# Attention and a squared-ReLU MLP on one core: a new order for the attention stage's list of steps, with other ranks, engine letters and buffer homes

## The chip, the cores and the metric

The kernel runs on one core of a Trainium2 chip. The core has five engines that run side by side, each through its own queue in order: TensorE (PE in the profile), VectorE (DVE), ScalarE (ACT), GpSimd (POOL) and SyncE (SP), which here only issues transfers. The time is device microseconds (us) of one execution, and the figure that counts is the median of several.

## The reference

Attention with a compressive memory, for 4 batches, 8 heads, 576 positions and 64 columns a head, and behind it an MLP on the 2304 x 512 result:

```python
scores = scale * q @ k.T                      # causal, S = 576, D = 64
a      = softmax(scores)                      # over the keys
local  = a @ v
q_p    = where(q > 0, q, exp(q) - 1) + 1
mem    = (q_p @ M_prev) / (q_p @ z_prev + 1e-6)
x      = g * mem + (1 - g) * local            # g = sigmoid(beta), one per head
h      = x @ w_in                             # 2304x512 @ 512x2048
y      = (s * relu(h) ** 2 + b) @ w_out       # 2304x2048 @ 2048x512
```

## The kernel before

**Stages.** PE does three things one after the other. First comes the attention stage: 16 pairs of heads (pair g is batch g // 4, heads 2p and 2p+1), and in among them the first 41 blocks of `x @ w_in`. It ends at 282 us. Then come the other blocks of `x @ w_in`, up to about 367 us, and then the product with `w_out` (lines 800 to 904). Only the first stage is planned from a list of steps; the other two are loops written out by hand.

**A pair in the attention stage.** Three *visits* of PE (four for pair 0) make the scores (`scores`, L383) in two halves of PSUM called S buffers. DVE masks them, copies them out and takes row minima (`red`, L390). ACT takes exponentials and row sums (`ex`, L396). DVE adds the sums and inverts them (L435, L436), and DVE or POOL scales the rows (`scale`, L402). Beside this the memory term is made from the q rows (`phi`: `RELU` L319 to L323, exponential L324, DVE L325, `ZMUL` L329, DVE L331 to L335, `PUTS` L342). PE transposes both in four *banks* (`bank`, L463) into PSUM buffers called T, of which there are four, each bank taking two. ACT or DVE copies the banks out (`copy`, L472 to L479). PE makes the pair's result (`second`, L514), and ACT and DVE split it into a high and a low part `xs` (L535, L536). `x @ w_in` is done in three matmuls of such parts (`mm1`, L580 to L582), and `w_in`, which arrives as 64-bit numbers, is turned into a high and a low part in 20 *pieces* (`convert`, L558 to L573; pieces 0 to 7 are 256 columns wide, the others 512).

**What sets the order.** `Plan.add` takes a step with an engine, a cost, a rank, what it reads and writes, and PSUM buffers that it takes and gives. `Plan.deal` then plays the steps through in a model of the engines: at each turn the engine that is free first takes the step with the lowest rank among those that are ready. The resulting order is written out as it is; each engine's queue on the chip holds the instructions in that order, and on the chip each waits for what it really needs. In the model a transfer lands 1.9 us after its last byte is sent, POOL's steps and the DVE steps marked `port` never overlap, and PE changes from blocks of `x @ w_in` ("full") to attention work when a ready attention step has waited `HOLD` or the ready ones add up to `WORK`; both have an early and a late value, and `TURN` is the model's time at which the late one begins.

**Matmuls that only keep PE running.** `warm(n, ps)` (L270) issues n matmuls of a zero tile; each is two instructions in the trace, all of line 272. `WARM` of them open the kernel. `FILL` has the number that follows each of pair 0's four visits. `Plan.waits` adds more wherever the model sees PE idle for over a microsecond and a PSUM buffer free.

**The numbers of a pair.** `AT[g]` is the rank r0 from which all ranks of pair g count: loads r0 - 4 to r0 - 1, `red` r0 + 0.1 - `UR`, `ex` r0 + 0.15, `scale` r0 + `RC`, transposes r0 + `RT`, copies r0 + `RT` + 0.1 - `UC`, result r0 + `RA`, `xs` r0 + `RX` - `UX`; `RPS` and `RQS` place the two halves of the memory term. `RELU`, `ZMUL`, `PUTS`, `COPY` and `SCAL` name the engine of a step for each pair (A, D, P for ACT, DVE, POOL; in `SCAL` one letter for each of the five row tiles, in `COPY` one for each bank), `HIGH` and `LOW` that of each piece's two parts. `W0` to `WS` are the ranks of the pieces, `WL` how far ahead of its rank a piece's load stands. `JOIN[g]` says which banks of a pair are transposed as one step (a: banks 0 and 3; b: banks 1 and 2; c: both). `HOME[m]` is the kind of PSUM buffer for block m, T or S. The first `EARLY` blocks of batch 0 run their first half as soon as pairs 0 and 1 are done.

All visits also write a common key `"visit"`, so that they stand in the list in the order of the pairs, whatever their ranks. The blocks of `x @ w_in` are chained in the same way, by `"seq"`.

Of the kernel before, what the change touches and what calls it, by code (L numbers as in the profile page):

```python
# [43 lines left out]
class Plan:  # L44
# [5 lines left out]
    LAT = 0.17  # L50
    RATE = 220.0e3
    SWITCH = {"full": 0.22, "row": 0.13, "col": 0.13}
    TURN = 80
    HOLD, WORK, WAIT = (2.5, 3), (0.5, 4), (0.15, 0.05)
    FREE = {"DVE": 0.05, "POOL": 0.10}

    def __init__(self, **pools):
# [20 lines left out]
    def deal(self):  # L78
        ready = {}
        clock = {}  # L80
        wire = port = 0.0
# [11 lines left out]
        while any(ready.values()):  # L93
            best = None
            for eng, some in ready.items():
# [16 lines left out]
                if eng == "PE":  # L112
                    late = t0 >= self.TURN
                    wait = 0.15 if mode == "full" else self.WAIT[late]
# [9 lines left out]
                t, s = min(now, key=lambda x: (x[1]["rank"], x[1]["n"]))  # L124
# [3 lines left out]
            t, s = best  # L128
# [7 lines left out]
                port = max(port, s["end"] - self.FREE[s["eng"]])  # L136
            if s["bytes"]:
                wire = max(wire, t) + s["bytes"] / self.RATE
                s["end"] = wire + 1.9
            for place, pool in s["take"]:  # L140
                f = self.free[pool]
                k = min((k for k in range(len(f)) if f[k] is not None), key=lambda k: f[k])
# [29 lines left out]
def attention_moe_kernel(  # L172
# [116 lines left out]

    plan = Plan(S=2, T=4)  # L290
    plan.idle = "TS", 0.3, lambda n, pool, k: warm(n, TB[k] if pool == "T" else SB[k])
    WARM, FILL = 7, (3, 4, 2, 6)
    UR, UC, UX = 0.6, 1, 0
    RP, RC, RT, RA, RX = 0.9, 0.5, 1.4, 2.4, 2.3
    RPS = [0.6, 0.6, 0.6, 0.4, -0.5, 0.6, 0.2, 0.4, ] + [0.4] * 8
    RQS = [0.7, 0, 0.9, 0.5, 0.9, -1.5, -1, -1, ] + [0.3] * 8
    RSR, WL = 0.6, 2
    RELU = "DPAAADDAPPAAAAAA"
    ZMUL = "DDPPDDDPPPPPPPPP"
    PUTS = "PDPDPDDDPPPPPPPP"  # L300
    COPY = ["AADA", "DAAD", "AAAD", "AAAA", "AAAA", "AADA", "AAAA", "DAAD", "DAAD", "AADA", ] + ["AAAD"] * 6
    SCAL = ["DPPPP", "PPPPP", "DPPPP", "DDDDD", "DPPPP", "DDPPP", "PPPPP", "PPPDD", "PPDDD", "PPPPP", ] + ["PPPPP"] * 6
    HIGH, LOW = "APAAAAAAAPAAAAAAPPPP", "DPDDDDPDDDDDPPDDDDDP"
    PARTS = "3232333222222222"
    AT = [-0.3, 1.8, 4.4, 5.7, 9.3, 10.8, 12.9, 16.2, 20.5, 22.5, 26.4, 27.1, 39.1, 40.0, 41.8, 46.8]
    W0, W1, W2, W3, WA, WB, WC, WD, WS = 5, 6.6, 6, 6.5, 8.5, 9, 12, 0.4, 0.4

    def phi(g):
        b, p = divmod(g, NP)
# [8 lines left out]
        if RELU[g] == "A":  # L318
            add("ACT", 0.72, lambda: nc.scalar.activation(PHR, q, AF.Relu), r0 + RPS[g], [("q", u)], ["phr"])  # L319
        elif RELU[g] == "D":  # L320
            add("DVE", 0.45, lambda: nc.vector.tensor_scalar(PHR, q, 0.0, None, ALU.max), r0 + RPS[g], [("q", u)], ["phr"], port=True)
        else:
            add("POOL", 0.88, lambda: nc.gpsimd.tensor_scalar(PHR, q, 0.0, None, ALU.max), r0 + RPS[g], [("q", u)], ["phr"])  # L323
        add("ACT", 0.72, lambda: nc.scalar.activation(q, q, AF.Exp), r0 + RPS[g] + 0.01, [], [("q", u)])  # L324
        add("DVE", 0.73, lambda: nc.vector.scalar_tensor_tensor(q, q, 1.0, PHR, ALU.min, ALU.add), r0 + RPS[g] + 0.1,  # L325
            ["phr"], [("q", u)], port=True)
        side = lambda c: (("POOL", nc.gpsimd), ("DVE", nc.vector))[c == "D"]
        ez, mul = side(ZMUL[g])
        add(ez, 1.54 if ez == "POOL" else 0.83, lambda: mul.tensor_mul(  # L329
            PHR, q, z.unsqueeze(1).to_broadcast([128, 5, 2, D])), r0 + RQS[g] + 0.01, [("q", u), ("z", u)], ["phr"], port=True)  # L330
        add("DVE", 0.73, lambda: nc.vector.tensor_reduce(n, PHR, AX.X, ALU.add), r0 + RQS[g] + 0.02, ["phr"], [("n", u)])  # L331
# [290 lines left out]
            tick()  # L622

    LEFT = 7
    HOME = "TTTTTTTTTTTSTTTSTTTTTSSSTSTTTTTTTTSSSTTTT"
    JOIN = "00000000c0000aa0"
    EARLY = 2
    MM = [(b, f) for b in range(B - 1) for f in range(NF - LEFT * (b == 2))]
    WRANK = [W0, W1, W2, W3] + [WA + WD * k for k in range(4)] + [WB + WD * k for k in range(4)] + [
        WC + WS * k for k in range(8)]  # L630
# [322 lines left out]
```

## Time and profile before

| | |
|---|---|
| time, median of 3 runs (lowest to highest) | 553.13 us (551.82 to 553.98) |
| the profiled execution: its time, and its span | 551.54 us, 549.8 us |
| PE busy, share of the span | 539.8 us, 98% |
| ACT busy, share | 398.8 us, 73% |
| DVE busy, share | 392.4 us, 71% |
| POOL busy, share | 273.2 us, 50% |

The span runs from the first to the last instruction; the 1.7 us by which the time is longer lie around it. An engine is busy while one of its instructions runs; PE's busy time also holds the matmuls that only keep it running. "Idle before" is time in which an engine stood still ahead of an instruction, with the engine that released it.

### The profile page before, as it was taken

Reading aid. Unit: us, or ns where it says so; the run is one execution under the profiler, and the core shown is the slowest. Engines: PE = TensorE matmul, PEld = TensorE weight load, DVE = VectorE, ACT = ScalarE, POOL = GpSimd, SP = SyncE. Lnnn points to the kernel's source line nnn. Section 1 sums busy time; section 2 is a strip of 40 time slices with the busy share of each in tenths; the row PEclk is TensorE's granted clock in tenths of the full one; section 3 lists DMA queues with packets and bytes.
Section 4 is the critical chain, followed back from the end, with each engine's and each line's share of the span. In section 5 each row is a group of like instructions: output and inputs, shape, how many; then the busy total and the mean of one; then the engine's idle time right before and its main releaser. Section 6 shows DMA issues by size and latency. Waiting matters only on the chain.

```text
span 549.8 us, 11492 instructions
## 1 busy us (share of the span) xinstructions
PE 539.8 (98%) x4104; PEld 445.5 (81%) x4104; DVE 392.4 (71%) x971; ACT 398.8 (73%) x877; POOL 273.2 (50%) x279
## 2 busy tenths in 40 slices
PE   9899999999999999999999999999999999999997
PEld 7666677777777777777788888889999999999996
DVE  5899999999666455234009979344798898888872
ACT  5999899974788747646325668969987977887840
POOL 3773454567756653454000000327578668768760
PEclk9999999999999999999999999999999999999999
DMA  6645686645444342321148574649335344353101
GB/s 184 197 141 162 195 267 189 219 152 173 134 165 131 101 136 98 106 78 45 58 142 356 168 252 153 204 159 301 106 107 163 117 128 150 106 163 116 39 30 38
DMA packets 56665, 81.50 MB, mean 148 GB/s; under 512 B 7584, under 2 KB 39072, under 8 KB 56608
## 3 DMA queue, kind: packets, MB, share of 16 engines
q1 hardware_dynamic: 54064, 78.63, 44.2%
q10 hardware_dynamic: 2544, 2.14, 1.2%
q8 instruction: 32, 0.52, 0.4%
q14 instruction: 25, 0.20, 0.1%
HBM read 57.15 MB, written 23.59 MB: 147 GB/s over the span
## 4 chain that ended last, share of the span: by engine, by line
PE 89%; DVE 7%; POOL 1%; DMA 1%; issue 1%; ACT 0%; DVEq 0%; POOLq 0%
PE yps L808 12%; PE yps L812 11%; PE sb L514 7%; PE sb L383 7%; PE tb L580 6%; PE hps L580 5%; PE hps L581 5%; PE hps L582 5%; PE tb L463 5%; PE yps L811 5%; PE yps L810 5%; PE tb L581 5%; PE tb L582 5%; DVE P L390 2%; PE tb L514 2%; PE sb L580 2%
## 5 line engine op out<-in xcount | busy, mean ns | idle before, releaser
L402 POOL TENSOR_SCALAR P<-P,sr,omg 128x576 f32<-128x576 f32 (+4 forms) x130 | 90.7, 712 | 56.2 <-DVE sr L436 21.6
L812 PE MATMUL yps<-rb,op 128*128 128x256 f32 x360 | 101.1, 281 | 0.0
L396 ACT ACTIVATE P<-P,mn 128x64 f32<-128x64 f32 (+4 forms) x160 | 88.7, 560 | 17.0 <-DVE mn L390 16.4
L390 DVE CUSTOM_DVE_ANT_0 P<-sb,mask 128x64 f32<-128x64 f32 (+4 forms) x160 | 71.4, 483 | 21.0 <-PE sb L383 20.8
L808 PE MATMUL yps<-rb,op 128*128 128x512 f32 x216 | 76.9, 396 | 0.0
L812 PEld LDWEIGHTS yps<-rb,op 128*128 128x128 f32 x360 | 67.9, 189 | 0.0
L788 POOL TENSOR_TENSOR sum<-src 128x512 f32<-128x512 f32 x10 | 13.0, 1296 | 103.4 <-ACT src L772 88.7
L383 PE MATMUL sb<-qk 64*128 64x288 f32 (+4 forms) x384 | 57.0, 409 | 0.2 <-DMA qk<-in_qk_t_dram 0.2
L796 POOL TENSOR_TENSOR op<-src,op 128x512 fp32r<-128x512 f32 x30 | 43.5, 1470 | 16.9 <-ACT op L795 16.8
L819 DVE TENSOR_TENSOR yu<-yu,yps 128x256 f32<-128x256 f32 x90 | 36.5, 414 | 19.8 <-PE yps L812 18.8
L463 PEld LDWEIGHTS tb<-ident,P 64*128 64x128 f32 x928 | 37.2, 139 | 14.6 <-issue 4.8
L808 PEld LDWEIGHTS yps<-rb,op 128*128 128x128 f32 x216 | 40.6, 188 | 9.0
L463 PE MATMUL tb<-ident,P 64*128 64x64 f32 x928 | 43.2, 227 | 3.3 <-DVE xs L536 1.3
L383 PEld LDWEIGHTS sb<-qk 64*128 64x128 f32 x384 | 35.7, 188 | 12.8 <-issue 6.8
L810 PE MATMUL yps<-rb,op 128*128 128x256 f32 x144 | 40.5, 281 | 0.0
L811 PE MATMUL yps<-rb,op 128*128 128x256 f32 x144 | 40.5, 281 | 0.0
L795 ACT CAST op<-src 128x512 fp32r<-128x512 f32 x50 | 30.3, 615 | 11.5 <-PE yps L812 9.8
L796 DVE TENSOR_TENSOR op<-sum,op 128x512 fp32r<-128x512 f32 x36 | 37.1, 1032 | 0.8 <-ACT op L795 0.7
L472 ACT COPY pt<-tb 128x512 f32<-128x512 f32 x58 | 31.2, 588 | 7.7 <-PE tb L463 7.5
L796 POOL TENSOR_TENSOR op<-w1H,op 128x512 fp32r<-128x512 f32 x24 | 34.9, 1484 | 0.0
L587 ACT ACTIVATE r<-hps 128x256 f32<-128x256 f32 x62 | 21.5, 388 | 16.4 <-DMA r_d<-r 13.3
L396 ACT ACTIVATION_READ_ACCUMULATOR P<-P,mn 128x1 f32 x160 | 31.2, 195 | 0.0
(172 smaller groups left out, 1550.0 us busy)
## 6 DMA issues: line engine op xcount, KB each, us to landing
r_d<-r SPq DMA_DIRECT2D x41, 256.0 KB, 2.3
src<-r_d SPq DMA_DIRECT2D x20, 512.0 KB, 4.6
qk<-in_qk_t_dram SPq DMA_DIRECT2D x15, 576.0 KB, 4.1
raw<-in_moe_w_out_dram SPq DMA_DIRECT2D x16, 512.0 KB, 6.8
w1H<-r_d SPq DMA_DIRECT2D x16, 512.0 KB, 4.5
xa<-in_moe_w_in_dram SPq DMA_DIRECT2D x12, 512.0 KB, 5.1
r_d<-r SPq DMA_DIRECT2D x48, 128.0 KB, 2.3
qs<-in_q_rows_dram SPq DMA_DIRECT2D x16, 320.0 KB, 3.7
```

The source lines that it names most:

```text
L383: nc.tensor.matmul(at(ps, j, o, n), lhsT=qk[rs, 128 * i:128 * i + 128], rhs=qk[rs, S + 64 + c0:S + 64 + c0 + n], start=True, stop=True, ti ...
L390: nc.vector.tensor_tensor_reduce(P[:, j, PB[i] + 64:PB[i] + 64 + n], at(ps, j, o, n), m, -SCALE, 3.0e38, ALU.add, ALU.min, mn[:, j, i:i + 1])
L396: nc.scalar.activation(pt, pt, AF.Exp, scale=-1.0, bias=mn[:, j, i:i + 1], accum_out=sm[:, j, i, 0:1])
L402: e.tensor_scalar(pt, pt, sr[:, j, i:i + 1], omg[:, h:h + 1], ALU.mult, ALU.mult)
L463: nc.tensor.transpose(TB[ps[h]][:, o[h]:o[h] + 64], P[rs, j, c:c + 128], ident[rs, rs], tile_position=(64 * h, 0))
L580: nc.tensor.matmul(ps, lhsT=wH[:, p, fs], rhs=xs[:, 0], start=p == 0, stop=False)
L581: nc.tensor.matmul(ps, lhsT=wH[:, p, fs], rhs=xs[:, 1], start=False, stop=False)
L796: (nc.gpsimd if m in ONPOOL else nc.vector).tensor_sub(L, x, H.bitcast(F32))
L808: nc.tensor.matmul(tile, lhsT=H, rhs=B, start=f == 0, stop=False)
L810: nc.tensor.matmul(ps, lhsT=H, rhs=B[:, 0], start=f == 0, stop=False)
L811: nc.tensor.matmul(ps, lhsT=H, rhs=B[:, 1], start=False, stop=False)
L812: nc.tensor.matmul(ps, lhsT=L, rhs=B[:, 0], start=False, stop=f == KF - 1)
```

## The change

The model of transfers lands them half a microsecond later (2.4 in place of 1.9 us behind the last byte), two rules for PE's change between kinds of work are loosened, pair 0's `FILL` matmuls are taken out, and nearly all ranks, engine letters and homes are replaced. With them `Plan.deal` makes another list. No step is added to the computation and none taken away, and the loops after the attention stage are the same.

```diff
-    TURN = 80
-    HOLD, WORK, WAIT = (2.5, 3), (0.5, 4), (0.15, 0.05)
+    TURN = 110
+    HOLD, WORK, WAIT = (2.5, 3), (1, 5), (0.15, 0.05)
...
-                s["end"] = wire + 1.9
+                s["end"] = wire + 2.4
...
-    WARM, FILL = 7, (3, 4, 2, 6)
-    UR, UC, UX = 0.6, 1, 0
-    RP, RC, RT, RA, RX = 0.9, 0.5, 1.4, 2.4, 2.3
-    RPS = [0.6, 0.6, 0.6, 0.4, -0.5, 0.6, 0.2, 0.4, ] + [0.4] * 8
-    RQS = [0.7, 0, 0.9, 0.5, 0.9, -1.5, -1, -1, ] + [0.3] * 8
-    RSR, WL = 0.6, 2
-    RELU = "DPAAADDAPPAAAAAA"
-    ZMUL = "DDPPDDDPPPPPPPPP"
-    PUTS = "PDPDPDDDPPPPPPPP"
-    COPY = ["AADA", "DAAD", "AAAD", "AAAA", "AAAA", "AADA", "AAAA", "DAAD", "DAAD", "AADA", ] + ["AAAD"] * 6
-    SCAL = ["DPPPP", "PPPPP", "DPPPP", "DDDDD", "DPPPP", "DDPPP", "PPPPP", "PPPDD", "PPDDD", "PPPPP", ] + ["PPPPP"] * 6
-    HIGH, LOW = "APAAAAAAAPAAAAAAPPPP", "DPDDDDPDDDDDPPDDDDDP"
-    PARTS = "3232333222222222"
-    AT = [-0.3, 1.8, 4.4, 5.7, 9.3, 10.8, 12.9, 16.2, 20.5, 22.5, 26.4, 27.1, 39.1, 40.0, 41.8, 46.8]
-    W0, W1, W2, W3, WA, WB, WC, WD, WS = 5, 6.6, 6, 6.5, 8.5, 9, 12, 0.4, 0.4
+    WARM, FILL = 7, (0, 0, 0, 0)
+    UR, UC, UX = 1.5, 2, 1
+    RP, RC, RT, RA, RX = 0.7, 0.5, 1.4, 2.0, 2.6
+    RPS = [0.6, 0.9, -0.5, 0.6, 0.6, 0.6, 0.2, 0.6, ] + [-2] * 8
+    RQS = [0, -1.5, 0.5, -1, 0.9, -1, 0.7, 0.3, ] + [0.9] * 8
+    RSR, WL = 0.6, 5
+    RELU = "APAAADPAADAAAAAA"
+    ZMUL = "PPPDDDDDDPPPPPPP"
+    PUTS = "PPPDPPPPDDPPPPPP"
+    COPY = ["AADD", "DAAD", "AAAD", "AAAA", "AAAA", "AAAA", "AAAA", "AAAD", "DDAD", "AAAD", ] + ["AAAD"] * 6
+    SCAL = ["PPPPP", "PPPPP", "DPPPP", "DDDDD", "DPPPP", "PPPDD", "DPPPD", "DDDDD", "DPPPD", "PPPDD", ] + ["PPPPP"] * 6
+    HIGH, LOW = "AAPAAAAAPPAAAPAPPPAA", "DPPDDPDPDDPDDDDDPDDD"
+    PARTS = "3232332223222222"
+    AT = [-1.4, 0.9, 5.1, 7.8, 12.2, 13.1, 15.5, 19.7, 24.3, 26.2, 29.8, 31.5, 47.5, 23.2, 53.5, 29.1]
+    W0, W1, W2, W3, WA, WB, WC, WD, WS = 4.5, 6.3, 6, 4, 8, 10, 14, 0.4, 0.6
...
-    HOME = "TTTTTTTTTTTSTTTSTTTTTSSSTSTTTTTTTTSSSTTTT"
-    JOIN = "00000000c0000aa0"
-    EARLY = 2
+    HOME = "TTTTTTTTTSTTTTTTTTTTTSSSSSTTSSSTSTTSSSTSS"
+    JOIN = "b0b00000b0caa0bb"
+    EARLY = 1
```

## Rows read from the trace of the kernel before

**Rows 1.** Busy time by stretch: start:end, length, each engine's busy us (instructions), clock, DMA.

```profile
4.63:61.00 56.37, 52.47 (x540) 38.17 (x541) 53.02 (x204) 48.77 (x147) 28.18 (x36) 1.00 0.56 171
61.00:282.00 221.00, 219.82 (x1862) 164.22 (x1859) 137.76 (x451) 153.31 (x407) 113.42 (x142) 1.00 0.43 139
...
50.00:61.00 11.00, 9.39 (x82) 7.17 (x79) 10.93 (x38) 8.62 (x24) 0.11 (x1) 1.00 0.47 132
```

**Rows 2.** The same view for line 272 alone: length, PE and weight-load busy us, clock.

```profile
0.00:4.63 4.63, 3.36 (x14) 3.06 (x14) 1.00 0.45 106
4.63:61.00 56.37, 12.60 (x82) 10.12 (x82) 1.00 0.56 171
...
50.00:61.00 11.00, 3.07 (x18) 2.31 (x18) 1.00 0.47 132
```

**Rows 3.** Timeline of PE: start us, us, operation, count [idle before, releaser].

```profile
5.40 0.94 PE L272 MATMUL tb<-w 128*128 128x128 f32 x6
6.26 0.81 PE L383 MATMUL sb<-qk 64*128 64x320 f32 x4
7.00 1.16 PE L272 MATMUL tb<-w 128*128 128x128 f32 x8
8.09 1.02 PE L383 MATMUL sb<-qk 64*128 64x448 f32 x4
...
66.94 0.50 PE L580 MATMUL tb<-xs,w0H 128*128 128x512 f32 x1
67.27 0.39 PE L581 MATMUL tb<-xs,w0H 128*128 128x512 f32 x1
...
274.99 0.50 PE L580 MATMUL tb<-xs,w0H 128*128 128x512 f32 x1
```

**Rows 4.** Timeline of DVE, the same columns.

```profile
7.12 0.49 DVE L390 CUSTOM_DVE_ANT_0 P<-sb,mask 128x320 f32<-128x320 f32 x1 [0.49 <-PE sb L383]
...
9.16 0.62 DVE L390 CUSTOM_DVE_ANT_0 P<-sb,mask 128x448 f32<-128x448 f32 x1 [0.46 <-PE sb L383]
...
10.32 0.53 DVE L402 TENSOR_SCALAR P<-P,sr,omg 128x64 f32<-128x64 f32 x2
...
24.02 0.17 DVE L332 SCALAR_TENSOR_TENSOR nrm<-nrm,gin 128x10 f32<-128x10 f32 x1
...
40.21 0.56 DVE L332 SCALAR_TENSOR_TENSOR nrm<-nrm,gin 128x10 f32<-128x10 f32 x1
```

**Rows 5.** DVE from 4.63 to 61 us by line: count, busy us, mean ns, idle before.

```profile
L402 DVE TENSOR_SCALAR P<-P,sr,omg 128x64 f32<-128x64 f32 (+4 forms) x14 | 5.2, 399 | 0.0
...
L329 DVE TENSOR_TENSOR phr<-qs,z 128x640 f32<-128x640 f32 x3 | 2.5, 821 | 0.0
...
L342 DVE TENSOR_TENSOR P<-qs,nrm 128x384 f32<-128x384 f32 (+1 forms) x4 | 2.2, 571 | 0.0
L571 DVE TENSOR_TENSOR w0L<-w,w0H 128x256 fp32r<-128x256 f32 x5 | 2.1, 419 | 0.0
...
L476 DVE COPY F<-tb 128x384 f32<-128x384 f32 x2 | 1.1, 548 | 0.0
...
L321 DVE TENSOR_SCALAR phr<-qs 128x640 f32<-128x640 f32 x1 | 0.5, 464 | 0.0
```

**Rows 6.** POOL from 4.63 to 61 us by line, the same columns.

```profile
L402 POOL TENSOR_SCALAR P<-P,sr,omg 128x448 f32<-128x448 f32 (+4 forms) x27 | 18.9, 711 | 22.4 <-ACT F L474 11.9 <-DVE sr L436 10.5
L329 POOL TENSOR_TENSOR phr<-qs,z 128x640 f32<-128x640 f32 x2 | 3.4, 1712 | 4.4 <-DVE qs L325 4.4
L342 POOL TENSOR_TENSOR P<-qs,nrm 128x384 f32<-128x384 f32 (+1 forms) x4 | 3.4, 874 | 0.5 <-DVE w L561 0.5
```

**Rows 7.** Timeline of ACT, just ahead of pair 3's last copy.

```profile
59.21 0.57 ACT L396 ACTIVATE P<-P,mn 128x320 f32<-128x320 f32 x1
```

**Rows 8.** Timeline of POOL.

```profile
24.48 5.66 POOL L402 TENSOR_SCALAR P<-P,sr,omg 128x448 f32<-128x448 f32 x9 [2.43 <-DVE sr L436]
...
36.82 3.93 POOL L402 TENSOR_SCALAR P<-P,sr,omg 128x320 f32<-128x320 f32 x6
```

## The prediction, made before the changed kernel ran

> **What bounds the kernel now.** I read the busy time by stretch first. From 61 to 282 us PE is busy 219.82 of 221.00 us [rows 1]; the loops behind that are not planned and stay as they are. A new list can therefore win little behind 61 us: 1.2 us of idle time and what PE spends on changing between kinds of work. Before 61 us it is otherwise. Of the 56.37 us from 4.63 on, PE stands idle for 3.90 (56.37 less 52.47) [rows 1], and 12.60 of its busy time are matmuls of the zero tile [rows 2]. So 16.5 us here are no work. The same row shows why: DVE is busy 53.02 of 56.37 us, ACT 48.77, POOL 28.18 [rows 1]. PE waits for the first four pairs to come through DVE and ACT. Once pair 3 is through, every block of batch 0 has its input and PE never starves again. That is the picture I work with: **the end moves by as much as pair 3 comes through earlier or later**, plus small change later. No view of waits names a load among what DVE, ACT or POOL waited for behind 5 us.
>
> **The change part by part.**
>
> *FILL.* It removes 15 warm calls, 30 instructions. They aren't all hidden: visit 1 stands behind six of them (5.40 to 6.26) and visit 2 behind eight, of 7.00 to 8.09 [rows 3], and DVE idles 0.49 and 0.46 us for just these two visits [rows 4]. Bounds: 0 (the planner puts matmuls of its own into the gaps) and -0.95. I take -0.9: the planner puts its own only where its model sees PE idle for over a microsecond, and both idle times of DVE are half of that.
>
> *Engine letters of pairs 0 to 3 and pieces 0 to 3.* What leaves DVE: pair 0's RELU (0.46), ZMUL (0.82) [rows 5] and two scalings of 64 columns (0.53 for both [rows 4]); pair 1's ZMUL (0.82) and two PUTS (0.57 each); piece 2's low part (0.42) [rows 5]. Sum 4.19. What comes to DVE: pair 0's bank 3, two copies of at most 0.55, and pair 3's ZMUL, 0.82 [rows 5]: 1.92. DVE is relieved of 2.3 us ahead of the point where PE stops starving. ACT's load stays about the same: it gets a RELU and a piece's high part, and loses two copies and another high part. POOL gets pair 0's ZMUL (1.71) and two scalings (0.71 each), pair 1's ZMUL (1.71) and two PUTS (0.87 each) and a low part (two inputs like a PUTS, so 0.87 too), and loses pair 3's ZMUL (1.71) [rows 6]: 5.7 us more on top of 28.2. It is idle half of the stretch [rows 1], which is the cover. If POOL stands on the path instead, up to 5.7 us are added. I take -2.3: DVE, at 94% busy, is the nearer limit. Bounds -2.3 and +5.7. The letters of pairs 4 to 9 move DVE work in both directions; by then PE is full, so nothing is counted.
>
> *Ranks.* Pair 4 goes from 9.3 to 12.2, while the pieces keep theirs within two units, and copies and `xs` come a unit earlier against their pair. So less of pair 4 stands ahead of pair 3's end. Directly ahead of pair 3's last copy ACT does an exponential of pair 4, 0.57 us [rows 7]. I take -0.6, that row. Bounds: 0, and -4.7, all that is no work between 50 and 61 us, where PE waits for pair 3 alone: 1.61 idle [rows 1] and 3.07 of zero tile [rows 2]. EARLY 1 lets only one block run half ahead; the other half's six matmuls of at most 0.5 us each [rows 3] then wait for pair 3 and leave up to 3.0 us to other work or to idling. That is the reason why I stay near the lower of the two bounds.
>
> *Loads.* The model's later landing and WL = 5 only move issues on SP. Pieces' loads now stand ahead of pairs' loads in SP's queue; one that waits for its buffer holds the pair loads behind it. Cost 0, since no engine waits for a load now; without that cover the price is the half microsecond of the model for each late load.
>
> *JOIN.* Eight pairs in place of three transpose joined banks. Pairs 0 and 2, ahead of 61 us, now do banks 1 and 2 as one step, which needs all four T buffers and both banks' inputs. Each may hold PE until one more scaling is done, 0.71 [rows 6]: bounds 0 and +1.4, and with nothing to decide between them I take +0.7.
>
> *TURN, WORK, HOME.* Behind 60 us there are 34 returns to blocks, the first at 66.94, the last at 274.99; the first matmul of each lasts 0.50 where the next lasts 0.39 [rows 3]. So all of them together cost 3.7 us, twice that if leaving costs as much. A late WORK of 5 in place of 4 may save a fifth of them, seven times 0.11 or 0.8 us; a later TURN gives some back. Bounds -1.2 and +0.5; I take -0.5. More blocks in S buffers keep visits waiting, but PE has other work then, up to the 1.2 us of idle time it shows there now.
>
> *AT of pairs 13 and 15.* Ranks of 23 and 29 let their memory term come early. Their scores can't overtake pairs 12 and 14 (the key "visit"). This is in the stretch where PE is full: 0.
>
> **Sum:** -0.9 - 2.3 - 0.6 + 0.7 - 0.5 = -3.6 us. Against the profiled execution, 551.54, that is 547.9; the median of the runs shown is 1.6 higher, 553.13, so the forecast is **549.5**. About half a per cent, 2.8 us, is what a measurement of this kernel can tell from no change; faster by that means under 550.4, slower means over 555.9.
>
> **Rivals.**
>
> *POOL and DVE get in each other's way (no change).* A small DVE step, L332, took 0.17 us at 24.02 [rows 4], when POOL was idle before 24.48 [rows 8], and 0.56 at 40.21 [rows 4], late in a POOL run of 36.82 to 40.75 [rows 8]. It ended when POOL did. If such steps never overlap POOL, what counts is the sum of both. DVE's ten groups of two inputs or of plain scaling (L402's 5.2 us the largest, L321's 0.5 the smallest [rows 5]) come to 24.8 us, and POOL to 28.2 [rows 1]: 53.0 of 56.4. The change takes 3.4 off the one and puts 5.7 on the other, 55.3. Then the relief of 2.3 is gone and up to 2.3 are added: -1.3 to +1.0, so 551.8 to 554.1. For it: the two rows. Against it: what counts is the order ahead of pair 3, and POOL's idle time lies partly where DVE does score rows, which don't collide. Chance 0.28.
>
> The Trainium skill (SBUF — State Buffer, "Who interferes with whom") says that a DVE instruction with two inputs in SBUF and a GpSimd one that reads SBUF exclude each other for the whole instruction. The pair of L332 rows agrees; by that rule the sum would be the rival's, 553.0 in its middle, and not 549.5.
>
> *POOL becomes the first pairs' path (slower).* From 24.48 POOL already runs nine scalings without a gap [rows 8], and the change queues pair 1's ZMUL and PUTS among them, behind pair 0's ZMUL. If all its 5.7 us lie on the path in place of DVE's relief, the sum is -0.9 - 0.6 + 0.7 - 0.5 + 5.7 = +4.4: 557.5. It decides from the point where over 4.1 of the 5.7 us lie on the path (then +2.8). For it: POOL takes twice DVE's time for the same step (1.71 against 0.82). Against it: its 22.4 us of idle time ahead of scalings [rows 6]. Chance 0.17.
>
> *PE's clock falls between the visits (slower or same).* The granted clock is 1.00, the upper level of 2.4 GHz, in every stretch [rows 1]. But the 14 matmuls that open the kernel take 3.36 us, 0.24 each [rows 2], against 0.86 for six later on [rows 3], 0.14 each. Without FILL, pair 0's and 1's first six visits, about 1 us each [rows 3], could take twice that, 6 us more, all in front of DVE: -3.6 + 6.0 = +2.4, 555.5. Against it: PE still has the visits, and the planner's own matmuls in longer gaps. Chance 0.06.
>
> The Trainium skill (TensorE: Matmul & The Clock Gate, Part 1) holds the array at half its clock unless it was busy of late, which speaks against taking FILL out. The slow first 14 matmuls agree with it; no row shows a later fall.
>
> *The order itself wins more.* If pair 4's work in front of pair 3 really goes, the ranks' term is -4.7 and not -0.6: -7.7, 545.4. For it: 16.5 us are there to be won. Against it: pieces now press in front of pair 3, too. Chance 0.11.
>
> **How the numbers follow.** My forecast has the other 0.38; its own range is 547.5 to 551.5, of which 0.06 of the chance lies over 550.4. Faster: 0.11 + 0.38 - 0.06 for its upper end = 0.43. Same: 0.28 + 0.06 and 0.03 of the clock's 0.06, less 0.03 for the first rival's ends, 0.34. Slower: 0.17 + 0.03 + 0.03 = 0.23. The range leaves out half of the largest win and of the largest loss each: 545 to 557.
>
> **What would show it.** In the changed trace the matmuls of line 272 from 4.63 us until PE is full, and idle time there, should sum to some 12 to 13 us in place of 16.5. Pair 3's L514, which now begins as the first stretch ends, should begin about 3 us before 61. DVE's two idle times of half a microsecond ahead of visits 1 and 2 should be gone. If POOL is the path, PE's transposes of pairs 0 and 1 will wait for L402 or L342; if POOL and DVE collide, POOL's and DVE's mean durations in that stretch will be longer; if the clock falls, early L383 rows will be twice as long. I am wrong if PE, behind the starved stretch, no longer runs without gaps, since I count nothing there.

## The result, and the profile after

The changed kernel takes 557.11 us (median of 6 runs, 555.95 to 558.01), the kernel before 552.58 beside it (6 runs, 551.50 to 554.23). The ratio is 1.0078, 95% interval 1.0055 to 1.0100. It is slower by 4.5 us; the forecast was 3.6 us faster, and its range ended at 557. The profiled execution took 556.89, its span 555.1.

The runs of before fall into two groups, near 551.7 and near 553.9 us, nearly all of them at a granted clock of 1.00, so their median moves with the share of each, from 551.63 to 552.58 in the sets used here; what parts the groups isn't shown. Every run of the changed kernel is longer than every run of before. Below, each ratio stands against runs of before on the same chip in the same set. Kernels of different sets are compared by median and by ratio, and where the two differ both are given.

Busy time by stretch, after (start:end, length, busy us of PE, PE's weight loads, DVE, ACT, POOL, each with instructions, then clock, DMA share, GB/s). It answers to [rows 1]; the first stretch runs from the first visit to the start of pair 3's result, which in before is at 61.61, a little behind the 61.00 of [rows 1]:

```profile
4.38:66.95 62.57, 52.71 (x519) 37.95 (x518) 54.62 (x202) 49.57 (x148) 32.85 (x44) 0.92 0.57 176
66.95:287.00 220.05, 219.55 (x1864) 164.67 (x1862) 141.57 (x455) 154.19 (x407) 93.03 (x128) 1.00 0.42 135
...
57.00:67.00 10.00, 7.31 (x60) 5.58 (x60) 7.17 (x27) 7.11 (x19) 2.09 (x3) 0.50 0.47 153
```

The same view for line 272 (PE, weight loads, clock, DMA), which answers to [rows 2]:

```profile
4.38:66.95 62.57, 10.51 (x65) 8.63 (x64) 0.92 0.57 176
```

Behind pair 3's result PE is as full as before, busy 219.55 of the 220.05 us of the second row. The loss lies ahead of it. Idle time and zero matmuls sum to 62.57 - 52.71 + 10.51 = 20.4 us, where before had 16.5 and the forecast 12 to 13. DVE was busy 54.62 us; before, up to 61.61 us, it was 53.63, and 2.3 us of work had been taken from it.

Read from PE's timeline of each kernel: the start of pair 0's visit 2 (the first L383 of 448 columns), of each pair's result (L514), and the end of the attention stage (first `hps` of L580):

| kernel | visit 2 | pair 0 | 1 | 2 | 3 | end of stage |
|---|---|---|---|---|---|---|
| before | 8.09 | 25.30 | 34.97 | 46.12 | 61.61 | 281.92 |
| after | 7.04 | 24.15 | 34.71 | 47.97 | 66.95 | 287.13 |
| after, own zero tile | 6.37 | 23.46 | 34.02 | 46.69 | 62.32 | 282.35 |
| before, own zero tile | 7.95 | 25.15 | 34.83 | 45.98 | 61.30 | 281.60 |

The start of visit 2 differs by up to 0.9 us between kernels whose lists begin alike, and by 2.6 us between two executions of one kernel (last section), so what lies between two results tells more than the results themselves.

Pair 0 is 1.15 us ahead of before, pair 2 is 1.85 behind, pair 3 5.3 behind. The last step is the large one. PE's timeline there, after (start, us, operation, count, [idle before, releaser]):

```profile
52.32 2.05 PE L272 MATMUL tb<-w 128*128 128x128 f32 x16 [0.99 <-DVE w L562]
54.30 0.27 PE L463 MATMUL tb<-ident,P 64*128 64x64 f32 x1
55.23 0.65 PE L463 MATMUL tb<-ident,P 64*128 64x64 f32 x13 [0.65 <-DVE xs L536]
56.52 0.28 PE L463 MATMUL tb<-ident,P 64*128 64x64 f32 x2 [0.64 <-DVE P L402]
58.55 0.87 PE L463 MATMUL tb<-ident,P 64*128 64x64 f32 x10 [1.76 <-DVE P L402]
59.35 1.22 PE L272 MATMUL tb<-w 128*128 128x128 f32 x4
60.50 1.11 PE L463 MATMUL tb<-ident,P 64*128 64x64 f32 x16
62.75 1.20 PE L272 MATMUL tb<-w 128*128 128x128 f32 x4 [1.14 <-ACT pt L472]
```

DVE's timeline over the same time:

```profile
51.84 0.76 DVE L562 SCALAR_TENSOR_TENSOR w<-xa,w 128x256 uint32<-128x256 uint32 x2
52.52 0.22 DVE L536 TENSOR_TENSOR x<-tb,x 128x64 fp32r<-128x64 f32 x1
54.41 0.43 DVE L564 SCALAR_TENSOR_TENSOR w<-xa,w 128x256 uint32<-128x256 uint32 x1 [1.68 <-PE tb L272]
54.75 0.75 DVE L536 TENSOR_TENSOR xs<-tb,xs 128x256 fp32r<-128x256 f32 x2
...
60.68 0.29 DVE L561 TENSOR_SCALAR w<-w 128x256 uint32<-128x256 uint32 x1 [1.07 <-PE tb L272]
```

The first row of PE holds the answer: the 16 clock-keeping matmuls read `w` and wait for DVE's write of `w`. `busy`, the zero tile of `warm`, is no tile of its own. Line 268 makes it a slice of a buffer into which `w_in`'s pieces are converted:

```python
    busy = WT[0][:, :128]
```

So each `warm` of the planner reads what L561 to L564 write. PE waits 0.99 us for an L562; then DVE's next L564 waits 1.68 us for the 16 matmuls. Behind it in DVE's queue stands the move of `xs` (L536), for which PE's transposes wait in turn (0.65). At 60.68 the same thing costs DVE 1.07 us. In the kernel before PE waited 0.4 us in all for this tile and DVE not at all: its list happened to keep zero matmuls and pieces apart.

### The profile page after: what moved, and what is told of

Its sections match the earlier page's. It is cut to its first block, busy times and chain, and to the rows that moved or that the text cites. A ratio compares the mean times of both kernels' runs of the same rounds, so it can differ in the third digit from the quotient of the medians.

```text
span 555.1 us, 11449 instructions
## 1 busy us (share of the span) xinstructions
PE 540.1 (97%) x4086; PEld 445.9 (80%) x4086; DVE 398.4 (72%) x976; ACT 400.6 (72%) x878; POOL 258.2 (47%) x273
## 4 chain that ended last, share of the span: by engine, by line
PE 89%; DVE 6%; ACT 3%; POOL 1%; issue 1%; DVEq 0%; ACTq 0%; POOLq 0%
PE yps L808 12%; PE yps L812 11%; PE sb L514 7%; PE sb L383 6%; PE hps L580 5%; PE hps L581 5%; PE hps L582 5%; PE tb L580 5%; PE yps L811 5%; PE yps L810 5%; PE tb L463 4%; PE tb L581 4%; PE tb L582 4%; PE sb L580 3%; PE sb L582 2%; PE sb L581 2%
## 5 line engine op out<-in xcount | busy, mean ns | idle before, releaser
L396 ACT ACTIVATE P<-P,mn 128x448 f32<-128x448 f32 (+4 forms) x160 | 88.4, 561 | 25.9 <-DVE mn L390 24.8
L402 POOL TENSOR_SCALAR P<-P,sr,omg 128x192 f32<-128x192 f32 (+4 forms) x120 | 76.5, 654 | 64.9 <-DVE sr L436 45.2
L390 DVE CUSTOM_DVE_ANT_0 P<-sb,mask 128x448 f32<-128x448 f32 (+4 forms) x160 | 70.8, 481 | 21.7 <-PE sb L383 21.5
L383 PE MATMUL sb<-qk 64*128 64x288 f32 (+4 forms) x384 | 58.5, 420 | 1.1 <-DVE mn L390 0.8
L383 PEld LDWEIGHTS sb<-qk 64*128 64x128 f32 x384 | 36.4, 194 | 15.4 <-issue 5.3
L463 PE MATMUL tb<-ident,P 64*128 64x64 f32 x928 | 41.2, 230 | 5.5 <-DVE P L402 2.4
L796 DVE TENSOR_TENSOR op<-sum,op 128x512 fp32r<-128x512 f32 x36 | 38.8, 1078 | 0.2
```

Of the source, the lines that this page charges most:

```text
L383: nc.tensor.matmul(at(ps, j, o, n), lhsT=qk[rs, 128 * i:128 * i + 128], rhs=qk[rs, S + 64 + c0:S + 64 + c0 + n], start=True, stop=True, ti ...
L390: nc.vector.tensor_tensor_reduce(P[:, j, PB[i] + 64:PB[i] + 64 + n], at(ps, j, o, n), m, -SCALE, 3.0e38, ALU.add, ALU.min, mn[:, j, i:i + 1])
L396: nc.scalar.activation(pt, pt, AF.Exp, scale=-1.0, bias=mn[:, j, i:i + 1], accum_out=sm[:, j, i, 0:1])
L402: e.tensor_scalar(pt, pt, sr[:, j, i:i + 1], omg[:, h:h + 1], ALU.mult, ALU.mult)
L463: nc.tensor.transpose(TB[ps[h]][:, o[h]:o[h] + 64], P[rs, j, c:c + 128], ident[rs, rs], tile_position=(64 * h, 0))
L796: (nc.gpsimd if m in ONPOOL else nc.vector).tensor_sub(L, x, H.bitcast(F32))
```

## The experiments

**1. A zero tile of its own, in both kernels** (`a_tile` from after, `b_tile` from before). One line each; the lists stay as they are.

```diff
-    busy = WT[0][:, :128]
+    busy = ap1.tile([128, 128], F32, name="zero")
```

> The changed kernel with its list kept to the letter; only the zero tile that the clock-keeping matmuls read is a tile of its own and no longer a slice of the buffer in which pieces of w_in are converted. Theory T (shared tile): in the changed kernel DVE's conversion waits 1.68 and 1.07 us for such matmuls, and PE 0.99 us for DVE; without the shared tile all three waits go, pair 3's result starts 2.5 to 4 us earlier than at 66.95 us, and the median is 553 to 555, against 557.1. Theory C (clock): PE idles all the same, the clock still falls to 0.5 near 57 us, and at most 1 us is won (556 to 557). Theory P (POOL and DVE exclude each other): the 2.10 us shift at 27 us stays as it is, 556 to 557.

> The kernel before with the same edit. Its trace shows only 0.2 and 0.2 us of PE waiting for ACT and DVE over the shared tile and no wait of DVE or ACT for such matmuls. Theory T: same, -0.5 to 0 us (552 to 552.6). If the shared tile cost the kernel before as well, 549 to 551.

Measured: after 552.37 (0.9992 of before, 0.9977 to 1.0007), before 551.61 (0.9976, 0.9963 to 0.9990). The one line takes 4.7 us off the changed kernel, by the median and by the ratio: all that it had lost. The waits between L272 and DVE's steps on `w` are gone. In `a_tile` the same 16 matmuls on PE, and the same L564 on DVE, start without one:

```profile
49.98 2.05 PE L272 MATMUL tb<-zero 128*128 128x128 f32 x16
```

```profile
51.38 0.41 DVE L564 SCALAR_TENSOR_TENSOR w<-xa,w 128x256 uint32<-128x256 uint32 x1
```

From pair 0's result to pair 3's it now takes 38.86 us in place of 42.80 (before: 36.31), which is 3.9 of the 4.7; another 0.7 lies ahead of visit 2, where executions differ by as much. What the prediction called the change, the new list, is then level with the kernel before and 0.8 us behind the one with the same repair. In a second set (run 5) the repaired kernel before was level with before (551.60, ratio 1.0001), so it isn't shown that the repair wins anything there.

**2. The same wait from its two other ends, in the changed kernel.** `a_no8` leaves out the 16 zero matmuls at 52.32 (`if n > 1 and free and n != 8`). `a_noshift` leaves out piece 0's shift L561, on which the first two column blocks of the MLP depend.

> The changed kernel with the shared tile, without the planner's 16 zero-tile matmuls at 52.3 us, which DVE's conversion and, behind it in its queue, pair 2's result part wait for. Theory T: DVE's wait of 1.68 us goes, 1.5 to 3 us off, 554 to 555.6, although nothing holds the clock any more. Theory C (the clock is what costs): the clock falls earlier, 557 to 559.

> The changed kernel with its list kept, but without piece 0's left shift (line 561; the output of the MLP's first two column blocks is not the reference's). On DVE this shift of 256 columns lasts 2.10 us at 27.07, where others of its size last 0.28, while POOL runs scalings and a product without a gap. Theory P: 2.0 us leave DVE's path and pair 3 comes through 1.5 to 2 us earlier, 555.1 to 555.6. Theory T: the later waits for the zero-tile matmuls absorb most of it, 556.3 to 557.1.

Measured: 555.29 (1.0055, 1.0042 to 1.0067) and 556.60 (1.0056, 1.0034 to 1.0078). Without the 16, DVE's wait of 1.68 is gone and the one of 1.07 is left; 1.8 us come back by the median (1.3 by the ratio), although the granted clock is 0.50 from 56 to 66 us and falls a first time at 32 to 36. Less work on DVE early, with both waits in place, brings 0.5 (1.2).

**3. How much the clock is worth.** In after the clock fell to 0.50, the lower level of 1.2 GHz. Two-microsecond stretches:

```profile
54.00:56.00 2.00, 1.22 (x18) 0.82 (x16) 1.59 (x5) 0.49 (x2) 0.00 (x0) 1.00 0.53 145
56.00:58.00 2.00, 0.28 (x2) 0.14 (x2) 2.00 (x5) 1.72 (x4) 0.73 (x1) 0.72 0.73 194
58.00:60.00 2.00, 1.45 (x13) 1.36 (x14) 1.61 (x6) 1.40 (x5) 0.00 (x0) 0.50 0.52 195
...
66.00:68.00 2.00, 2.00 (x14) 0.88 (x12) 0.94 (x3) 2.00 (x8) 1.43 (x2) 0.72 0.58 209
```

It falls also with the zero tile apart, from 54 to 62. `a_more` makes the planner's 16 zero matmuls near 50 us 28; `a_less` leaves out two groups of four near 55 us, both with the own tile. `b_nofill` takes FILL alone out of the kernel before.

```diff
-            n = int((b["start"] - a["end"] - 0.4) / cost)
+            n = {8: 14}.get(n0 := int((b["start"] - a["end"] - 0.4) / cost), n0)   # a_more
...
-            if n > 1 and free:
+            if n > 1 and free and not 53 < a["end"] < 56:                          # a_less
...
-  lambda v=v, free=free: warm(FILL[v], TB[free[0]])
+  lambda: None                                                                   # b_nofill
```

> The changed kernel with a zero tile of its own (552.37 us), with the planner's 16 matmuls of the zero tile near 50 us made 28. There PE's granted clock falls to 0.5 from 55 to 61 us, after 2.4 us of idle time. Theory C (the clock costs what is left): the clock stays at 1.00, pair 3's result starts 1 to 3 us before 62.3, 549.5 to 551.4. If the fall is hidden by DVE, which is busy throughout: 552 to 553, with or without the fall.

> The changed kernel with a zero tile of its own, without the two groups of four zero-tile matmuls at 56.3 and 58.5 us, which run at half clock between pair 3's transposes (1.2 us each, PE not idle before or behind them). If PE is the path there: 1 to 2.4 us off, 550 to 551.4. If the copies on ACT behind the transposes are the path: 552 to 552.6.

> The kernel before with its list kept; the fixed clock-keeping matmuls behind pair 0's visits are not issued (30 instructions fewer). Theory F, as forecast: DVE's idle times of 0.49 and 0.46 us ahead of visits 1 and 2 go, -0.3 to -0.9 us, 551.7 to 552.3. Theory C (these matmuls hold the clock): the clock falls below 1.00 before 20 us and the time is 1 to 3 us longer, 553.6 to 555.6. If DVE has other waits behind: 0.

Measured: 551.69 (0.9989, 0.9980 to 0.9998), 552.99 (1.0010, 0.9999 to 1.0021) and 551.79 (0.9980, 0.9967 to 0.9993). Against `a_tile`, with 28 the clock falls for 4 us instead of 8 and the time is 0.7 lower by the median (0.2 by the ratio); from pair 2's result to pair 3's it takes 14.58 us in place of 15.63. With eight fewer the time is 0.6 higher (1.0), but in that profile the clock also fell at 32 to 38 us, ahead of anything that the edit touches, so the difference can't be put down to the eight. Without FILL the clock does fall in the place that the rival named. PE in `b_nofill`:

```profile
12.74 3.79 PE L383 MATMUL sb<-qk 64*128 64x448 f32 x16 [1.48 <-DVE mn L390]
```

This visit lasts 2.11 with FILL. Visit 2 starts at 7.04 in place of 8.09, and from there to pair 0's result it takes 17.9 us in place of 17.2: of the 1.05 us that FILL gives back, the slow visit takes 0.7. At 56 to 62 us the clock falls once more (0.79, 0.50, 0.86 in steps of two), and pair 3's result starts at 61.81, no earlier than before's 61.61. The kernel is 0.4 us faster by the median, 1.1 by the ratio; the profile doesn't show where.

**4. FILL and the own tile together** (`b_tile_nofill`).

> The kernel before with a zero tile of its own and no fixed matmuls on zeros between the first pair's score visits; no step has another place. If the two add (-0.5 to -0.9 and -0.8 to -0.4 us against the kernel before): 551.2 (550.6 to 551.6), the fastest so far. Rival: the granted clock falls near 13 us as it did without the fixed matmuls alone, and the first pair's matmuls at half clock take back what the 24 matmuls free: 551.6 to 552.2.

Measured: 551.38 (0.9993, 0.9983 to 1.0003), 0.2 under `b_tile` by the median, and by the ratio not under it. That the two add up isn't shown. The profile, with the clock at 1.00 throughout, is of the fastest run (550.21); nine of the twelve runs have a mean clock of 0.993 or 0.994.

**5. The letters by themselves, each way.** `b_letters` gives pairs 0, 1, 3 and pieces 1, 2 in the kernel before (own tile, old list) to the engines that the change names; `a_letters` puts the old letters into the new list (own tile), at the new places. No step moves.

```diff
-        ez, mul = side(ZMUL[g])
+        ez, mul = side(ZMUL[g])[0], side({0: "P", 1: "P", 3: "D"}.get(g, ZMUL[g]))[1]   # b_letters
+        ez, mul = side(ZMUL[g])[0], side({0: "D", 1: "D", 3: "P"}.get(g, ZMUL[g]))[1]   # a_letters
...
```

> The kernel before with a zero tile of its own (551.61 in its run) and its own list of steps, but pairs 0, 1 and 3 and pieces 1 and 2 done by the engines that the change's letters name: pair 0's RELU on ACT, its first scalings and multiplications on POOL, its last bank's copies on DVE; pair 1's multiplications on POOL; pair 3's on DVE; piece 1's high part on ACT, piece 2's high and low parts on POOL. The forecast's theory: DVE is relieved by the 2.3 us that the prediction summed and the end moves with it, 549.3 (548.5 to 550.2). Rival: POOL's blocks in a row hold DVE's instructions up by what they relieve, and the rest reaches pair 3 only in part, so 551.6 to 554. Rival of the list: the letters bring about a third of 2.3, 550.8 (550.4 to 551.3).

> The changed kernel with a zero tile of its own (552.37 in its run), the new list and its places kept, but the letters of before for the same steps: RELU of pair 0 on DVE, multiplications of pairs 0 and 1 on DVE, of pair 3 on POOL, pair 0's first scalings on DVE, its last bank's copies on ACT, pieces 1 and 2 as before. The forecast's theory: 2.3 us of work go back to DVE and the end is later by as much, 554.7 (553.8 to 555.5). Rival: with POOL's blocks gone DVE runs its own work at full speed, no change or up to 1 us earlier, 551.4 to 552.4. If only a third of DVE's work reaches the end: 553.1.

Measured: 554.07 (1.0040, 1.0025 to 1.0054) and 554.76 (1.0044, 1.0027 to 1.0061). In the new list the old letters cost 2.4 us by the median and 2.9 by the ratio; the forecast's theory had 554.7.

In the old list the new letters cost as much instead of bringing it. But the profile of `b_letters` shows half-speed matmuls until 10 us, so it and its base ran once more, as `b_letters2` and `b_tile2`:

> The same kernel as in the run of the letters in the old list, once more. In that run's profile PE's matmuls stayed at half speed until about 10 us (the first eight score matmuls of the second visit group took 1.44 us where the base had 0.81), which put pair 0's result 1.7 us later before any letter could act. Theory that the letters cost time at the old places: with an opening as fast as the base's, pair 3's result is still 1.5 to 3 us behind that of the base, and the median 1.5 to 3.5 us above it. Rival, that the late opening was the cost: pair 3's result within 0.7 us of the base and the median within 1 us.

> The base of it, the kernel before with a zero tile of its own, once more in the same set: 551.2 to 552.0 as before. If PE's opening at half speed comes by chance in any kernel, some runs are 1.5 to 3 us longer; then the lowest times are to be compared as well as the medians.

Measured: 553.90 (1.0038, 1.0026 to 1.0051) against 551.60 (1.0001, 0.9988 to 1.0013). The cost of 2.3 us (2.0 by the ratio) stays. With an opening like that of `b_tile`, pair 0's result now starts at 24.32, 0.8 earlier, and pair 1's at 36.66, 1.8 later; pair 3's is at 63.49. POOL in `b_letters2`, and behind it in `b_tile`:

```profile
19.36 1.40 POOL L342 TENSOR_TENSOR P<-qs,nrm 128x384 f32<-128x384 f32 x2
20.72 1.54 POOL L329 TENSOR_TENSOR phr<-qs,z 128x640 f32<-128x640 f32 x1
25.01 1.41 POOL L402 TENSOR_SCALAR P<-P,sr,omg 128x448 f32<-128x448 f32 x2 [2.75 <-DVE sr L436]
26.38 0.83 POOL L342 TENSOR_TENSOR P<-qs,nrm 128x384 f32<-128x384 f32 x1
27.20 1.60 POOL L402 TENSOR_SCALAR P<-P,sr,omg 128x192 f32<-128x192 f32 x3
28.77 0.61 POOL L342 TENSOR_TENSOR P<-qs,nrm 128x256 f32<-128x256 f32 x1
29.36 4.34 POOL L402 TENSOR_SCALAR P<-P,sr,omg 128x320 f32<-128x320 f32 x7
```

```profile
24.34 7.87 POOL L402 TENSOR_SCALAR P<-P,sr,omg 128x448 f32<-128x448 f32 x12 [2.44 <-DVE sr L436]
```

At the old places pair 1's `PUTS` stand in the middle of POOL's scalings, which end at 33.70 and not at 32.21; PE's waits for them grow from 1.2 to 2.3 us. Another part of pair 1's delay in `b_letters2` is the clock, 0.57 at 32 to 36 us. Pair 1's last visit there, and behind it in `b_tile`:

```profile
33.70 3.03 PE L383 MATMUL sb<-qk 64*128 64x448 f32 x16
```

```profile
32.79 2.11 PE L383 MATMUL sb<-qk 64*128 64x448 f32 x16
```

`b_letters` has the cost without this fall: from pair 0's result to pair 3's it takes 38.42 us in place of 36.15, and 1.16 of that lies ahead of pair 1's. For this part it is the rival "POOL becomes the first pairs' path", in a list that was not made for these letters. A letter has no price of its own; it has one in a list.

**6. The landing of loads** (`a_land`: own tile, 1.9 us again; the list is dealt anew from it).

```diff
-                s["end"] = wire + 2.4
+                s["end"] = wire + 1.9
```

> The changed kernel with a zero tile of its own and the landing of loads set back from 2.4 to 1.9 us, so that the list is dealt anew from that. The forecast's theory: the engines hardly wait for loads and the later landing only moves orders, so the same within what another order brings, 551.5 to 553.5. Rival: 2.4 us is nearer to the loads' true landing and the earlier dealing puts steps ahead of loads that have not come, so DVE or PE waits for loads in the first 30 us and the time is 554 to 557.

Measured: 564.67 (1.0234, 1.0215 to 1.0252), outside both ranges. PE's waits for loads are 0.7 us in all (0.6 with 2.4), and pair 3's result starts at 63.26, 0.9 later than in `a_tile`. The other 11 us or more come behind it:

```profile
63.26:296.20 232.94, 226.95 (x1892) 168.53 (x1890) 144.76 (x455) 154.84 (x407) 98.66 (x128) 1.00 0.44 144
```

In `a_tile` the same stretch takes 220.03, busy 219.51, without zero matmuls; here PE idles 5.5 us more, 4.1 us of its busy time are zero matmuls, and the same 1864 other instructions take 3.4 us longer. One load is late (in `a_tile` L319 never waits for one). From the timelines of ACT, DVE and PE:

```profile
182.60 0.74 ACT L319 ACTIVATE phr<-qs 128x640 f32<-128x640 f32 x1 [3.09 <-DMA qs<-in_q_rows_dram]
```

```profile
184.19 0.83 DVE L325 SCALAR_TENSOR_TENSOR qs<-qs,phr 128x640 f32<-128x640 f32 x1 [6.26 <-ACT qs L324]
```

```profile
186.14 1.13 PE L383 MATMUL sb<-qk 64*128 64x320 f32 x8 [1.99 <-DVE xs L536]
```

ACT waits for q rows, DVE for ACT, and PE for the `xs` that stands behind in DVE's queue; from 180 to 195 us PE idles 2.8 us. So the rival was right in kind for a part, at 182 us and not in the first 30. Half a microsecond in the model decides between two lists that differ by 12 us; what makes the rest of it is open.

**7. Where the new places lose.** With the repair the letters bring what I counted, and the total is still level; so the places lose about 3 us. Two were suspected, each moved by itself in the finished list of `a_tile`: the six early matmuls of `x @ w_in` ahead of pair 2's result (`a_mm1`), and piece 0's shift L561 ahead of pair 1's copies (`a_shift`). `a_tile_noshift` leaves that shift out (the same column blocks as above); `a_both` moves both, `a_all` has the 28 zero matmuls as well.

```diff
-        for step in plan.deal():
+        steps = plan.deal()
+        at = lambda n: next(i for i, x in enumerate(steps) if x.get("n") == n)
+        for a, b in [(432, 230)]:          # a_mm1; a_shift: (86, 148)
+            s = steps.pop(at(a))
+            steps.insert(at(b) + 1, s)
+        for step in steps:
             step["fn"]()
```

> The changed kernel with a zero tile of its own, without piece 0's left shift (the output of the MLP's first two column blocks is not the reference's). With the shared tile this won 0.5 us. Theory P (POOL holds DVE up at 27 us and this reaches the end once the later waits are gone): 550.4 to 551. If it is hidden even so: 551.9 to 552.4.

> The changed kernel with a zero tile of its own (552.37), and the first half of the first early matmuls (six matmuls of L580 to L582 that stand ahead of pair 2's result and wait 0.70 us for a copy of ACT) put right behind that result. Theory that the new places lose their time on PE: pair 2's result starts 1.6 us earlier and pair 3's and the end move with it by 0.8 to 1.6, so 550.8 to 551.6. Rival, that DVE is what pair 3 waits for: only fewer clock-keeping matmuls are behind it, pair 3's result within 0.3 of 62.32 and the time 552.0 to 552.6.

> The changed kernel with a zero tile of its own (552.37), and DVE's shift of piece 0 (L561, 2.09 us at 26.39 while POOL runs, ahead of the moves and copies for which PE waits 1.20 us) put behind pair 1's copies, where POOL stands idle. Theory of POOL and DVE: it lasts 0.3 us there instead of 2.09, PE's wait of 1.20 shrinks below 0.3 and pair 1's result is 1.0 to 1.8 us earlier; as leaving the instruction out brought 0.66, the end moves by 0.4 to 1.2, 551.2 to 552.0. Rival: it is as long wherever it stands, or another DVE instruction is held in its place by POOL's run, 552.2 to 552.6.

> Both moves, of the early matmuls and of piece 0's shift, in the changed kernel with a zero tile of its own. If the two places are where the new list loses and add up: 549.6 to 551.2, with pair 3's result at 60.0 to 61.0. If DVE alone sets pair 3: as the shift moved alone.

> Both moves and 28 clock-keeping matmuls instead of 16 near 50 us. If the clock's fall near 55 us costs 0.5 to 0.7 as in the run with 28 alone: 0.5 to 0.7 below the run with both moves, so 549.0 to 550.7, faster than both kernels. Rival: with pair 2's result earlier the gap on PE is longer, the 28 are not enough and the clock falls all the same, equal to the run with both moves.

| kernel | median | ratio, interval | pair 1 | pair 2 | pair 3 | from pair 0 to 3 |
|---|---|---|---|---|---|---|
| `a_tile` | 552.37 | 0.9992, 0.9977 to 1.0007 | 34.02 | 46.69 | 62.32 | 38.86 |
| `a_tile_noshift` | 551.71 | 0.9986, 0.9977 to 0.9995 | 33.80 | 46.48 | 61.99 | 37.87 |
| `a_mm1` | 551.80 | 0.9988, 0.9971 to 1.0005 | 36.06 | 46.97 | 61.98 | 38.16 |
| `a_shift` | 550.81 | 0.9972, 0.9958 to 0.9986 | 34.27 | 46.94 | 61.34 | 37.00 |
| `a_both` | 550.91 | 0.9966, 0.9951 to 0.9981 | 34.16 | 45.72 | 61.42 | 37.19 |
| `a_all` | 550.44 | 0.9959, 0.9943 to 0.9975 | 34.04 | 45.59 | 60.67 | 36.57 |

The shift in `a_tile` and then in `a_shift`, from DVE's timelines:

```profile
26.39 2.09 DVE L561 TENSOR_SCALAR w<-w 128x256 uint32<-128x256 uint32 x1
```

```profile
28.36 0.23 DVE L536 TENSOR_TENSOR x<-tb,x 128x64 fp32r<-128x64 f32 x1 [0.99 <-PE tb L463]
...
31.16 0.35 DVE L561 TENSOR_SCALAR w<-w 128x256 uint32<-128x256 uint32 x1
```

With one step moved by 5 us the time is 1.1 us lower by the ratio, 1.6 by the median: the step's 2.09 us become 0.35, at the end of POOL's run (until 31.37), and from pair 0's result to pair 3's it takes 37.0 us in place of 38.9 (before: 36.3). Not all of that is the shift. Up to pair 1's result 0.6 us are won (0.9 in `a_tile_noshift`), since DVE now waits 0.99 for PE there; from pair 1's to pair 2's, nothing. The other 1.2 us lie between pair 2's result and pair 3's (14.40 us where it was 15.63). There PE's rows are alike up to the last wait for DVE and differ behind it, in `a_tile` and then in `a_shift`:

```profile
55.46 0.87 PE L463 MATMUL tb<-ident,P 64*128 64x64 f32 x10 [1.71 <-DVE P L402]
56.26 1.22 PE L272 MATMUL tb<-zero 128*128 128x128 f32 x4
```

```profile
55.70 0.55 PE L463 MATMUL tb<-ident,P 64*128 64x64 f32 x10 [1.71 <-DVE P L402]
56.19 0.71 PE L272 MATMUL tb<-zero 128*128 128x128 f32 x4
```

The ten transposes start 8.8 us behind pair 2's result in both. From them to pair 3's result it takes 6.86 us in `a_tile`, where the clock from 54 us on, in steps of two, is 0.77, 0.50, 0.50 and 0.52, and 5.64 in `a_shift`, with 1.00, 0.81, 0.50 and 0.84. So these 1.2 us are a later fall of the clock; that moving the shift brought it about isn't shown, and with the shift left out it fell as in `a_tile`. Over the runs with a mean clock of 0.995 to 0.997 the medians are 551.96 (`a_tile`, 6 runs), 550.93 (left out, 5) and 550.88 (moved, 11): the shift behind POOL is worth about 1 us either way.

The early matmuls are the other case: with them out of the way pair 2's result is 1.2 us earlier in `a_both` than in `a_shift`, and pair 3's is not (61.42, 61.34). There DVE sets the end, as the rival of that run had it: the ten transposes that wait for its scaling start at 55.59 and 55.70. In the profile of `a_mm1` alone the clock fell to 0.57 at 32 to 36 us, ahead of the moved step, which made pair 1 late, and stayed at 1.00 behind; so its 0.3 us at pair 3's result can't be put down to the move.

`a_all` is the fastest kernel run here, 1.5 us under before by the median and 2.3 by the ratio. Its eleven runs all lie under the lowest of the 34 of before beside it (550.76 and 551.12), and in its profile the clock doesn't fall. `JOIN` was not tried by itself.

## Why the prediction was wrong

**The step that failed** stands in the part on FILL: "the planner puts matmuls of its own into the gaps", at no cost. I read matmuls of line 272 as time to be won and never asked what they read. [rows 3] showed it: their operand is `w`, as is the result of L561 to L564. The cost is 4.7 us, more than the whole of the sum and of the other sign. Neither a term nor a rival had this wait. Without it the forecast would have failed all the same: with the repair the changed kernel is level with before (552.37 and 552.15), not 3.6 us below. The terms that were mis-sized there are the ranks and JOIN.

**The picture** was right. The end moved as pair 3's result did (+5.34 and +5.21 us), and from there to the end of the stage it took 220.3 us before, 220.2 after and 220.0 to 220.8 in all the others but `a_land`.

**FILL, -0.9.** Right at its place: DVE's two idle times between the visits are gone, and visit 2 starts 1.05 us earlier. In the old list 0.7 of that is given back within pair 0, by the slow visit; alone FILL brought 0.4 to 1.1 us by the times, and nothing at pair 3's result in the profile.

**Letters, -2.3.** Right in size at the new places (2.4 to 2.9 by the times, 1.8 from visit 2 to pair 3's result in the profiles), wrong as a term that holds in any list (+2.0 to +3.5 at the old places, over two runs).

**Ranks and JOIN, -0.6 and +0.7.** This pair was mis-sized. The new list with the old letters is 2.4 to 3.1 us behind before; no run has ranks or JOIN alone, so that is what the list as a whole costs. The new letters bring it back. Of what they can't bring, about 1 us is held by the shift behind POOL and 0.2 (`a_more`, by the ratio) to 1.2 (between two profiles) by the clock near 57 us. The rest of the forecast's 3.6 is open.

**TURN, WORK, HOME, -0.5.** At most 0.3 (220.3 to 220.0 us, above).

**Loads, 0.** PE waits for loads 0.2 us before and at most 0.7 in the others. But the landing also decides which list is dealt, which I priced at nothing, and in the list dealt with 1.9 a load was late by 3.09 us (run 6).

**The rivals.** With the repair the time is 552.37, inside the first rival's 551.8 to 554.1, and rows of its kind are in the trace. In after, by line, from 4.38 to 66.9 us:

```profile
L325 DVE SCALAR_TENSOR_TENSOR qs<-qs,phr 128x640 f32<-128x640 f32 x5 | 5.0, 992 | 0.3 <-ACT qs L324 0.3
L561 DVE TENSOR_SCALAR w<-w 128x256 uint32<-128x256 uint32 x8 | 4.0, 505 | 1.1 <-PE tb L272 1.1
L562 DVE SCALAR_TENSOR_TENSOR w<-xa,w 128x256 uint32<-128x256 uint32 x8 | 3.7, 476 | 0.1
```

Before, the means were 816, 275 and 418 ns: 0.9 + 1.8 + 0.5 = 3.2 us more on DVE, where 2.3 had been taken off. These three lines were picked because they grew; L332, on which the rival rested, fell from 319 to 179 ns (0.6 us less). `a_shift` shows for one of these steps that undoing it gives time back; for the others it is argued. POOL as the path was not what happened in the new list, but in the old one with the new letters it was a part of the cost (1.1 of 2.3 us). The clock's fall was right in kind and wrong in place: not between the first visits, where it fell only in the old list without FILL (run 3), but near 57 us, where PE stood still.

## What to carry to other kernels

Matmuls that only keep PE running are instructions with an operand, and need a tile that nothing else ever writes; look up what their operand is called in the trace before counting them as free. Where engines share a resource, a step's price depends on what runs beside it: moving one small DVE step out of POOL's run brought about 1 us, and the same letters that brought 2.4 us in one list cost 2.0 in the other. And where a planner deals the list, a change of its numbers can't be priced term by term; take the finished list and move single steps. Before a difference between two profiles is put down to an edit, their granted clocks are to be compared stretch by stretch: of the 1.9 us by which `a_shift` is shorter than `a_tile` from pair 0's result to pair 3's, 1.2 were a later fall of the clock.

## What the hardware showed that was not expected

**A DVE step can be held through several POOL instructions.** DVE and then POOL in the changed kernel:

```profile
26.34 0.17 DVE L332 SCALAR_TENSOR_TENSOR nrm<-nrm,gin 128x10 f32<-128x10 f32 x1
...
27.07 2.10 DVE L561 TENSOR_SCALAR w<-w 128x256 uint32<-128x256 uint32 x1
```

```profile
22.52 5.12 POOL L402 TENSOR_SCALAR P<-P,sr,omg 128x448 f32<-128x448 f32 x9
27.61 1.41 POOL L342 TENSOR_TENSOR P<-qs,nrm 128x384 f32<-128x384 f32 x2
28.99 2.26 POOL L402 TENSOR_SCALAR P<-P,sr,omg 128x576 f32<-128x576 f32 x3
```

The shift has one input and takes 0.28 us elsewhere. Here it began 0.6 us before the end of nine scalings, lasted through both instructions of L342, which started after it, and ended at 29.17, 0.15 us after them. The Trainium skill (SBUF — State Buffer, "Who interferes with whom") has a one-input `tensor_scalar` among the steps that can take the pair of ports shared with GpSimd, and blocks the later one for the whole of the other's instruction. The trace agrees with the block; that it outlasts the instruction in progress is this trace's. Not every step is held: L332, with two inputs, took 0.17 us within the same nine scalings.

**PE's first matmuls come up to speed at different times in the same program.** PE in `b_letters`, then the clock over two of these microseconds in the view of busy time:

```profile
5.83 1.65 PE L272 MATMUL tb<-zero 128*128 128x128 f32 x6
7.41 1.44 PE L383 MATMUL sb<-qk 64*128 64x320 f32 x4
```

```profile
6.00:8.00 2.00, 2.00 (x8) 1.69 (x10) 1.00 (x9) 1.60 (x8) 0.00 (x0) 1.00 0.54 142
```

The same rows took 0.94 and 0.81 us before [rows 3] and 0.94 and 0.81 in `b_letters2`. They are nearly twice as long here although the clock column reads 1.00, so in the first 10 us the durations are the surer sign. It moved pair 0's result by 2.6 us between two executions of one kernel (26.89 and 24.32).

**The clock falls in some executions of a list and not in others.** In `a_no8`, `a_less` and `a_mm1` it fell at 32 to 36 us, and pair 1's last visit took 3.7 to 3.8 us; in after, `a_tile` and `a_more`, whose lists are the same up to there, it stayed at 1.00 and the visit took 2.11. In all six PE had stood idle for 1.2 us just before, waiting for DVE's L536. With the shift moved or left out in the repaired kernel that wait is 0.3 us, and none of those four profiles has the early fall.

**The lower clock near 57 us cost 1 to 2 us.** In `a_tile` it lasted 8 us. PE's rows from the last wait for DVE to pair 3's result took 6.86 us there and 5.20 in `a_mm1`, with the clock at 1.00: 1.7 us between the profiles. More zero matmuls, with 4 us at the lower level, changed the median by -0.7 us. In the wait itself PE stood idle for 1.7 us in both, so there the clock had no say. The Trainium skill (TensorE: Matmul & The Clock Gate, Part 1) holds the array at half its clock unless it was busy of late; the fall in after between 56 and 58 us, a stretch in which PE worked 0.28 us of 2, agrees.
